# Window attention, forward and backward, on one core: from feature-major tiles with broadcast weights to token-major tiles with four shifts or four feature quarters on the partitions

## The chip, the cores and the metric

The kernel runs on one core of a Trainium2 chip. Times are device microseconds of one execution. The times of all the runs quoted are medians, and each ratio comes with a 95% interval.

## The reference, cut to what matters

One transformer layer (LayerNorm, window attention, LayerNorm, GELU feed-forward, residuals), and the gradients of its input and all its weights for a given output gradient. There are 2048 tokens of 512 features in 32 heads of 16; each token attends to 8 keys, 0, 2, ... 14 tokens back.

```
W, dil = 8, 2
idx = pos[:, None] - (jnp.arange(W) * dil)[None, :]        # masked where negative
kg, vg = k[:, :, idx], v[:, :, idx]                        # heads, tokens, 8, 16
logits = einsum("bhsd,bhswd->bhsw", q, kg) * scale
attn = softmax(logits)
o = einsum("bhsw,bhswd->bhsd", attn, vg)
h = x + o @ wo
h2 = h + gelu(LN(h) @ w1 + b1) @ w2 + b2
outputs: h2 and its vjp with respect to x, wqkv, wo, w1, b1, w2, b2
```

Attention thus has two dot products over the 16 features of a head (the logits; in the backward pass the gradient of the weights) and four weighted sums over the window of 8 (the output, dV, dQ, dK).

## The kernel before

q, k and v lie feature-major: a partition is one of 16 features of one of 8 heads, tokens run along the row, and a shift by 2 tokens is an offset in the row. An attention weight has to be multiplied into all 16 features of its head, so it must be repeated on 16 partitions. The weights are transposed, stored to DRAM, and read back 16 times over by a transfer with a leading step of zero:

```
def put_wh(eng, d_t, n, col0, src):                 # store of the transposed weights
    for b in range(2):
        d0 = d_t[0:H, 0:1]
        eng.dma_start(out=_ap(d0, [[n, 4], [W * n, H], [1, src.shape[-1]]], ...), in_=src[:, b, :])

def bcast(eng, out_t, d_t, g, n, w0):               # 16 copies, 8 heads, one row each
    b = d_t[8 * g:8 * g + 8, w0 * n:(w0 + WH) * n]
    eng.dma_start(out=..., in_=_ap(b, [[0, DH], [W * n, 8], [1, WH * n]]))
...
def b_gv(c):                                        # dV, one of the four sums
    for g in range(G):
        ps = acc(...)
        for w0 in (0, WH):
            bc = bl.tile([P, WH, HB], BF16, tag="bc", bufs=5)
            bcast(sync, bc, attn_b[c], g, HB, w0)
            nc.vector.tensor_tensor(out=bc[:], in0=bc[:], in1=over_w(gos[c][:, g, :], HB), op=ALU.mult)
            gather(ps, bc, w0, True)                # four 128x128 identity matmuls
```

The dot products multiply q by the shifted k on DVE and sum 16 partitions with matmuls of 8 columns.

## Time and profile before

| | before |
|---|---|
| time, median of 2 runs | 926.27 us (925.79 to 926.75) |
| first stage (forward) | 375.1 us |
| second stage (feed-forward backward) | 191.4 us |
| third stage (attention backward, dW1, dWo) | 297.3 us |
| fourth stage (dWqkv) | 60.4 us |
| start of the third stage to its first window sum | 15.6 us |

The stages are cut in the trace by events: the first matmul of the feed-forward backward pass, its last dW2 matmul, the last output of the LayerNorm gradient, and the end. The prediction below uses round bounds a microsecond or two away.

### The profile page before, as it was taken

How to read it: one execution, taken by the hardware profiler on the slowest of the kernel's cores; microseconds unless marked ns; L12 is line 12 of the kernel's file. 1: busy time of each engine (PE TensorE's matmuls, PEld its weight loads, DVE VectorE, ACT ScalarE, POOL GpSimd, SP SyncE). 2: the span in 40 equal slices, each digit the busy share in tenths (PEclk: the TensorE clock that was granted, in tenths of full speed). 3: DMA queues.
4: the chain of work that ended last, by engine and by line, in shares of the span. 5: the costliest groups of instructions: out<-in, count | busy, mean ns of one | idle time of the engine just before them, and what ended most of it. 6: DMA issues, size and time to landing. Idle time of an engine off the chain costs nothing.

```text
span 924.2 us, 12961 instructions
## 1 busy us (share of the span) xinstructions
PE 759.3 (82%) x4946; PEld 373.9 (40%) x4946; DVE 560.8 (61%) x914; ACT 442.3 (48%) x608; POOL 252.8 (27%) x342
## 2 busy tenths in 40 slices
PE   1855877779779688999999997599699799888498
PEld 1533434334334233444454544254345345333243
DVE  5538247765673636579878863739749649777200
ACT  3543534753734645688787764132352342343211
POOL 6321211540431657244343212302102110100400
PEclk9966787999989998999999999689899989999799
DMA  9445384673491899965565524997885966984651
GB/s 326 155 152 191 103 245 155 208 285 111 143 307 76 317 318 312 258 216 162 170 206 174 186 79 137 271 282 228 230 233 149 257 187 183 244 235 149 232 222 40
DMA packets 64764, 187.86 MB, mean 203 GB/s; under 512 B 9981, under 2 KB 23166, under 8 KB 64702
## 3 DMA queue, kind: packets, MB, share of 16 engines
q0 software_dynamic: 34144, 114.41, 37.5%
q1 hardware_dynamic: 30558, 72.63, 28.1%
q8 instruction: 38, 0.62, 0.3%
q14 instruction: 24, 0.20, 0.1%
HBM read 119.74 MB, written 67.23 MB: 202 GB/s over the span
## 4 chain that ended last, share of the span: by engine, by line
PE 29%; DVE 14%; issue 13%; DMA 12%; ACT 6%; POOL 4%; ACTq 0%; DVEq 0%; POOLq 0%
DMA bv<-attn_b 5%; PE psq L747 5%; PE psw L698 4%; DMA bg<-gl_b 4%; PE psy L674 4%; PE psw L496 3%; PE psg L531 2%; PE psk L624 1%; PE psx L552 1%; PE psv L624 1%; DVE bv L638 1%; DVE bg L658 1%; ACT bu L522 1%; PE pswo L709 1%; DVE by L523 1%
## 5 line engine op out<-in xcount | busy, mean ns | idle before, releaser
L364 PE MATMUL psf<-ln2T,w 128*128 128x512 bf16 x224 | 63.0, 426 | 19.4 <-ACT u L366 19.4
L624 PEld LDWEIGHTS <-ident 128*128 128x128 bf16 x384 | 37.3, 99 | 64.7 <-issue 19.9
L330 DVE TENSOR_TENSOR bc<-bc,v 128x2048 bf16<-128x2048 bf16 x32 | 38.8, 1222 | 36.4 <-DMA bc<-attn_f 36.3
L698 PE MATMUL psw<-h1tm,ln2a 128*128 128x512 bf16 (+1 forms) x256 | 59.2, 355 | 1.2 <-ACT ow L701 1.2
L674 PE MATMUL psy<-wqkvT,gt 128*128 128x512 bf16 x192 | 54.7, 415 | 5.3 <-DVE lua L475 5.2
L600 DVE TENSOR_TENSOR bp<-go,bv 128x2048 bf16<-128x2048 bf16 x32 | 36.8, 1221 | 36.3 <-ACT go L595 36.3
L299 DVE TENSOR_TENSOR pr<-q,k 128x2048 bf16<-128x2048 bf16 x32 | 37.3, 1219 | 35.0 <-ACT q L283 30.5
L531 PE MATMUL psg<-goutT,w2T 128*128 128x512 bf16 x224 | 57.9, 379 | 0.1
L638 DVE TENSOR_TENSOR bv<-bv,go 128x2112 bf16<-128x2112 bf16 x32 | 39.7, 1253 | 29.9 <-DMA bv<-attn_b 27.0
L382 PE MATMUL ps<-w,g 128*128 128x512 bf16 x224 | 53.8, 388 | 3.9 <-ACT u L366 2.1
L747 PE MATMUL psq<-gqa,ln1a 128*128 128x512 bf16 x192 | 44.5, 397 | 11.3 <-DMA gqa<-gq_d 11.3
L496 PE MATMUL psw<-gout,gtm 128*128 128x512 bf16 x224 | 53.1, 379 | 0.0
L281 PE MATMUL psq<-ln1T,wqkv 128*128 128x512 bf16 x192 | 49.7, 410 | 4.1 <-ACT ln1T L217 3.7
L552 PE MATMUL psx<-w1T,gh 128*128 128x512 bf16 x224 | 52.3, 379 | 0.5 <-DVE luf L475 0.5
L332 PE MATMUL pso<-bc,ident 128*128 128x512 bf16 x128 | 37.4, 419 | 9.3 <-DVE bc L330 9.3
L402 ACT COPY wT<-ptw 128x1024 bf16<-128x1024 bf16 (+1 forms) x23 | 22.4, 975 | 44.8 <-DMA w1T_d<-wT 15.3
L364 PEld LDWEIGHTS <-w 128*128 128x128 bf16 x224 | 23.4, 107 | 50.6 <-issue 34.3
L366 ACT ACTIVATE u<-psf,b1c 128x512 bf16<-128x512 f32 x56 | 37.1, 687 | 13.7 <-PE psf L364 9.3
L657 DVE TENSOR_TENSOR bh<-bg,bk 128x2048 bf16<-128x2048 bf16 x32 | 38.5, 1218 | 8.4 <-DMA bg<-gl_b 6.9
L372 ACT ACTIVATE s<-z 128x1024 bf16<-128x1024 bf16 x28 | 29.4, 1054 | 28.9 <-DVE z L370 16.3
L533 DVE CUSTOM_DVE_ANT_0 gh<-psg,by 128x512 bf16<-128x512 f32 x56 | 37.3, 686 | 8.2 <-PE psg L531 7.3
L624 PE MATMUL psv<-bv,ident 128*128 128x512 bf16 x128 | 34.7, 415 | 7.6 <-DVE bv L638 7.6
(206 smaller groups left out, 1625.1 us busy)
## 6 DMA issues: line engine op xcount, KB each, us to landing
bv<-attn_b SPq DMA_DIRECT2D x32, 528.0 KB, 6.7
bg<-gl_b SPq DMA_DIRECT2D x32, 528.0 KB, 11.5
bc<-attn_f SPq DMA_DIRECT2D x32, 512.0 KB, 11.4
x_d<-u POOLq DMA_DIRECT2D x28, 256.0 KB, 5.5
s_d<-s POOLq DMA_DIRECT2D x28, 256.0 KB, 4.2
g_d<-g POOLq DMA_DIRECT2D x28, 256.0 KB, 4.3
bu<-x_d POOLq DMA_DIRECT2D x28, 256.0 KB, 3.7
bs<-s_d POOLq DMA_DIRECT2D x28, 256.0 KB, 4.4
```

Source lines behind the costliest of these rows:

```text
L281: nc.tensor.matmul(ps[:], lhsT=wqkv[:, dc, jt * P:(jt + 1) * P], rhs=ln1T[:, dc, :], start=(dc == 0), stop=(dc == DC - 1))
L330: nc.vector.tensor_tensor(out=bc[:], in0=bc[:], in1=back_w(v[:, g, PAD:HB], CH, w0), op=ALU.mult)
L364: nc.tensor.matmul(ps[:], lhsT=w1[:, dc, ft * P:(ft + 1) * P], rhs=ln2T[:, dc, :], start=(dc == 0), stop=(dc == DC - 1))
L382: nc.tensor.matmul(ps[:], lhsT=gs[ft // 2][:, ft % 2, j * P:(j + 1) * P], rhs=w2[:, ft, :], start=(ft == 0), stop=False)
L496: nc.tensor.matmul(ps[:], lhsT=gtm[:, t, :], rhs=gout[t // TC][:, t % TC, :], start=(t == 0), stop=(t == NT - 1))
L531: nc.tensor.matmul(ps[:], lhsT=w2T[:, dc, ft * P:(ft + 1) * P], rhs=gT[:, dc, :], start=(dc == 0), stop=(dc == DC - 1))
L552: nc.tensor.matmul(ps[:], lhsT=gh1[ft // 2][:, ft % 2, j * P:(j + 1) * P], rhs=w1T[:, ft, :], start=(ft == 0), stop=(ft == FT - 1))
L624: nc.tensor.matmul(ps[:], lhsT=ident[:], rhs=src[:, w, o:o + CH], start=(w0 + w == 0), stop=(w0 + w == W - 1))
L638: nc.vector.tensor_tensor(out=bc[:], in0=bc[:], in1=over_w(gos[c][:, g, :], HB), op=ALU.mult)
L674: nc.tensor.matmul(ps[:], lhsT=gts[c][sel][:, g, j * P:(j + 1) * P], rhs=wqkvT[:, sel * G + g, :], start=(n == 0), stop=(n == NJ - 1))
L698: nc.tensor.matmul(ps[:, 0:nf * P], lhsT=ln2a[:, t // TC, t % TC, dc * P:(dc + 1) * P], rhs=tmx[:, t, 0:nf * P], start=(t == 0), stop=(t = ...
L747: nc.tensor.matmul(ps[:], lhsT=ln1a[:, t // TC, t % TC, dc * P:(dc + 1) * P], rhs=gqt[:, t // TC, t % TC, :], start=(t == NT - 1), stop=(t ...
```

## The change

The intent is to drop the 96 broadcasts and the long identity matmuls. q, k, v and the weights are kept token-major in DRAM. A tile's 128 partitions are 4 x 32 rows of 64 tokens. For a weighted sum the four are four shifts of the same rows; for a dot product they are the four feature quarters. A matmul with a 128 x 32 selector then adds the four, and four such matmuls fill the 128 partitions of a PSUM tile.

```
-    def bcast(eng, out_t, d_t, g, n, w0): ...
-    def gather(ps, src, w0, sh): ...               # 128x128 identity matmuls
-    def logits(lg, pr, g, w0): ...                 # 8-column matmuls
+    def half_rows(ap2d, c, f, pad=0):
+        return _ap(ap2d, [[2 * n, Q4], [TPR * n, PR], [1, 2 * n]], ...)
+    def put_rows / get_rows                        # q, k, v, go, gl, attn; x, outputs: leading 4
+    def row4(pool_, d_t, t0, nj, name, tag, bufs, shift):
+        for j0 in range(0, nj, 5):
+            nn = min(5, nj - j0)
+            sync.dma_start(out=t_[:, j0:j0 + nn, :],
+                           in_=_ap(d_t[:, :], [[abs(shift) * n, Q4], [TPR * n, PR], [1, nn * n]], ...))
+    def att4 ...                                   # weights, 128 B pieces, 4 transfers of 32 partitions
+    def feat4 ...                                  # feature quarters, 256 B pieces, 4 transfers
+    def dots(...):                                 # DVE 128x4096 products, then
+        nc.tensor.matmul(lg[PR * n:PR * n + PR, ...], lhsT=sel4[:], rhs=pr[...])
+    def wsum(...):                                 # DVE 128x2048 products, then
+        nc.tensor.matmul(ps[PR * n:PR * n + PR, :], lhsT=sel4[:], rhs=prs[wh][:, n, :], ...)
...
-    b_ga(3); b_sm(3); b_gv(3)                      # then the loop, with take(wg, ...) between
+    b_go(0); take(wg, 1); b_go(1); b_ga(0); take(wg, 1); b_go(2); b_ga(1)
+    for c in range(NC): take(wg, 1); b_sum(c, 2); take(wg, 1); b_sum(c, 0); ...
```

dW1 goes in halves of 256 columns (448 matmuls for 256).

## The prediction

> **What bounds the kernel now.** I read the page's shares first, then a table of stretches that I cut where the stages change, then the costliest groups, then the DMA issues and the DMA rows of two short windows.
>
> ```profile
> PE 759.3 (82%) x4946; PEld 373.9 (40%) x4946; DVE 560.8 (61%) x914; ACT 442.3 (48%) x608; POOL 252.8 (27%) x342
> ...
> 0.00:374.00 374.00, 275.82 (x1804) 135.89 (x1805) 211.66 (x349) 186.28 (x250) 140.26 (x195) 0.88 0.64 213
> 374.00:566.50 192.50, 183.93 (x1189) 92.99 (x1188) 141.96 (x324) 143.13 (x178) 57.45 (x78) 1.00 0.57 172
> 566.50:865.00 298.50, 255.07 (x1763) 125.61 (x1761) 207.16 (x241) 105.45 (x169) 43.15 (x54) 0.93 0.78 218
> 865.00:924.00 59.00, 44.51 (x192) 19.42 (x192) 0.00 (x0) 7.47 (x13) 11.92 (x16) 0.88 0.47 174
> ```
>
> The columns of the stretches are their length, the busy time of PE, PEld, DVE, ACT and POOL, the granted clock, the DMA share and GB/s. Four stages follow each other: forward (374 us), FFN backward (192.5), attention backward with the dW1 and dWo products (298.5), dWqkv (59). The change lies in the first and the third. The third is nearly full on PE (255 of 298.5 us, 85%), and DVE (69%) and DMA (0.78) are not far behind: no single wait can be taken away for much.
>
> ```profile
> L330 DVE TENSOR_TENSOR bc<-bc,v 128x2048 bf16<-128x2048 bf16 x32 | 38.8, 1222 | 36.4 <-DMA bc<-attn_f 36.3
> L638 DVE TENSOR_TENSOR bv<-bv,go 128x2112 bf16<-128x2112 bf16 x32 | 39.7, 1253 | 29.9 <-DMA bv<-attn_b 27.0
> L332 PE MATMUL pso<-bc,ident 128*128 128x512 bf16 x128 | 37.4, 419 | 9.3 <-DVE bc L330 9.3
> L624 PE MATMUL psv<-bv,ident 128*128 128x512 bf16 x128 | 34.7, 415 | 7.6 <-DVE bv L638 7.6
> L290 PE MATMUL ga<-ind,bp 128*128 128x8 bf16 x512 | 17.6, 167 | 3.7 <-DVE bp L600 3.5
> ```
>
> The reader sees the work that the change re-shapes: products at 1.22 us for 2048 columns, sums over the window as 512 identity matmuls (pso, psv, psq, psk, 0.27 us each, 139.7 us together), 1024 eight-column matmuls for the dot products, and DVE waiting for the broadcasts.
>
> The last view settled the number for me: two stores of the same size and packet size, 128 KB in 128 pieces of 1 KB.
>
> ```profile
> DMA  0000000001311222333333222237515144788798
> ...
> attn_b<-aTa POOLq DMA_DIRECT2D x2, 128.0 KB, 6.1
> ...
> DMA  6992780799989794000000000870000000000000
> ...
> out_dram<-o SPq DMA_DIRECT2D x4, 128.0 KB, 1.7
> ```
>
> The first two lines are of 55 to 62 us, where the transposed weights attn_f and attn_b are stored; their DRAM pattern starts with a dimension of 4 (four steps of w or h, then 32 heads, then a row). For about 2 us the DMA share is 2 to 3 tenths. The last two are of 205 to 214 us, with output stores of 128 partitions x 1 KB: the share is 7 to 9 tenths while they run, and they land in 1.7 us instead of 6.1. In the DMA records an output store's 128 packets take 0.49 us with 12 in flight on average (267 GB/s); an attn_f store's 128 packets take 2.42 us with 3.4 in flight (54 GB/s). The second attn_f store was issued 0.6 us after the first and its packets began only when the first's had ended: both seem to use the same four engines.
>
> **What the Trainium skill says.** "DMA: Bandwidth & Descriptors", section "Why a DMA increments its semaphore by 16 and not by 1": the number of engines of a DMA is the largest k up to 16 that divides the slowest dimension of both patterns, and one issued from SP takes the lowest-numbered k. The 54 against 267 GB/s above agree. The same page, "Specifications", asks for at least 512 B per piece; here 512 B packets took 29 ns and 1 KB packets mostly 46, so small pieces cost more per byte but are not ruinous. "VectorE: DVE Perf Modes", "The perf-mode tier table": a bf16 tensor_tensor of 2048 takes 1224 ns; here 1219 to 1222. "TensorE: Matmul & The Clock Gate", "Part 3: Packing small matmuls": three column tiles of 32 columns at N=512 ran 2.38 times as fast; no run here shows it yet.
>
> **The change part by part.**
> DVE: the attention products keep their number of elements. 64 dot products of 2048 columns become 32 of 4096 (64 x 1.22 = 78 us against 32 x about 2.3 = 74), and 128 weighted products stay 128 (32 x 1.22, 32 x 1.25 and so on, 154 us together), of 2048 instead of partly 2112 columns, worth 2 us. The innermost runs are contiguous (32 or 128 elements), so I keep the rate. Softmax parts are unchanged. DVE gains some 6 us, all beside other work.
>
> PE: 512 identity matmuls (139.7 us) become 512 of 32 output columns, and 1024 small ones (34.9 us) become 256 of 512 columns. If four column tiles overlap about 3 times (an estimate from the page's 2.38 for three), the 768 cost 768 x 0.216 / 3 = 55 us instead of 175: 120 us less PE time, some 80 of it in the third stage, whose PE load falls to about 175 of 298. If they don't overlap, 768 x 0.216 = 166 us and nothing is gained. dW1 in halves of 256 columns is the same number of columns, a few us more of weight loads.
>
> DMA, bytes: the 96 broadcasts (50.6 MB) and 12 chunk reads (6.5 MB) go. In their place: 64 transfers of the four-shift rows, each 128 x 5,120 B = 655 KB (41.9 MB); 8 x 2 quarter-feature tiles (12 MB in 256 B pieces, 47,000 of them); 16 weight tiles (4.2 MB in 128 B pieces, 34,000). The bytes do not fall. At my estimate of 19 and 14 ns a packet (from 29 ns at 512 B and 46 at 1 KB) the small pieces cost 56 and 30 us of each engine over the kernel.
>
> DMA, engines: here I expect the damage. The four-shift read has the DRAM pattern 4 shifts x 32 rows x 5 KB against 128 partitions, so it runs on 4 engines, always the same, as attn_f did. A packet of 5,120 B: 4 KB took 159 ns at its quickest and 7 KB 272, so about 198 ns; attn_f's packets came every 2.42 x 4 / 128 = 76 ns per engine where an undisturbed one takes 46, so I add 30. 32 packets x 228 ns = 7.3 us per transfer, 14.6 us for a half chunk, for which DVE then has four products, 4 x 1.22 = 4.9 us: DVE will wait.
> Third stage: 48 transfers x 7.3 = 350 us on those four engines. The rest of their load: the stage has 234 us of packets per engine now, of which 122 are broadcasts and 23 chunk reads, leaving 89; plus 28 and 23 for the small pieces, 8 for the stores of go and gl, 22 for the dx stores, which also get a leading 4 and go out from SP; less 15 for less crowding. 350 + 155 = 505 us. The stage cannot end before these engines have done this, and of 298.5 us it becomes about 500: plus 200 us.
> First stage: 16 x 7.3 = 117 us; x read twice in 16 pieces of 256 KB with a leading 4, 3.8 us each, 60; out_0 in 8 such stores, 30; small pieces 36; what stays of the 239 us there now without the broadcasts (62) and the old x and output pieces (17), 160. Sum 403 us against 374: plus 35, since some of it lies at the wrong time.
> Second stage: unchanged. Fourth: its reads get 4 KB rows instead of 1 KB, worth perhaps 2 us of an 11 us wait.
> Sum: 926 + 200 + 35 - 2 = 1159; I say 1155.
>
> **The rivals.**
> (a) The four-shift reads spread over 16 engines after all (the lowering regroups the dimensions, or reads behave otherwise than the stores I have seen). Then 48 x 655 KB at the 200 GB/s of the broadcasts is 157 us in the third stage, PE falls to about 175 and DVE (205) is the bound: some 240 us instead of 298, with 5 or 10 gained in front. That makes about 865. Against it stand the two stores with exactly this pattern.
> (b) Confined, but the engines run nearer their best (198 ns) and the rest of the traffic falls between: 48 x 6.3 = 304 plus 120, a stage of 440; forward as it was: about 1075.
> (c) Confined, and the SP queue in its order makes it worse: it also carries output stores that wait for ACT (72.8 us in the stage now) and weight tiles that wait for a round trip of the softmax through DRAM; with two or three row buffers the four engines then stand idle at times: stage 560, forward plus 80, about 1270.
> (d) Column tiles don't overlap: with the engines of (a) busy elsewhere, PE stays at 255 and the time near 920; under my main theory it changes nothing, as PE has room.
>
> **Range and chances.** Confinement I hold for about nine in ten. Within it the spread is that of (b) and (c). Range 1000 to 1270 with 1155 in the middle of the confined cases; faster by over 2% 0.10 (a), within 2% 0.03 (d with a), slower 0.87.
>
> **What would show it.** Right: the four-shift reads land after 7 us or more each while the mean DMA share in the third stage is low (about 505 / 500 on four engines but near 150 / 500 on twelve, so 0.45 to 0.5 on average), DVE's longest waits are for these tiles, PE's share of the span falls below 70%, and the FFN backward stage keeps its 192 us. PE: groups of the 32-column matmuls with about 70 ns busy each show the overlap, 216 ns its absence. Wrong: landings of 3 to 4 us and a DMA share of 0.8 in the third stage mean (a); DVE products well over 1.22 us (or 2.4 for 4096 columns) mean that the broadcast operand lost its rate, which I don't count; a first stage longer than 420 us means that the trip of q, k and v through DRAM before the first dot product costs more than I allow.

## More of the kernel before

The order of the backward attention is: dot products and softmax gradient of the last chunk, its dV, and only then, between the later parts, some dW1 products taken from a list (`take`) as filler for PE.

From the page of the kernel before: how many packets the transfers were cut into, the chain that ended last by engine, and the issues of the broadcasts (number, size, median us from issue to landing).

```profile
DMA packets 64764, 187.86 MB, mean 203 GB/s; under 512 B 9981, under 2 KB 23166, under 8 KB 64702
...
PE 29%; DVE 14%; issue 13%; DMA 12%; ACT 6%; POOL 4%; ACTq 0%; DVEq 0%; POOLq 0%
...
bv<-attn_b SPq DMA_DIRECT2D x32, 528.0 KB, 6.7
bg<-gl_b SPq DMA_DIRECT2D x32, 528.0 KB, 11.5
bc<-attn_f SPq DMA_DIRECT2D x32, 512.0 KB, 11.4
```

The chain is PE first and DMA fourth: transfers are many, but the work is mostly there when it is wanted. Half a megabyte lands 7 to 12 us after its issue, several of them in flight.

## The result and the profile after

| | before | after |
|---|---|---|
| time, median | 926.27 us | 1253.41 us (1251.89 to 1254.93, 2 runs) |
| first stage | 375.1 | 468.0 |
| second stage | 191.4 | 190.1 |
| third stage | 297.3 | 532.8 |
| fourth stage | 60.4 | 62.2 |
| third stage's start to first window sum | 15.6 | 71.9 |

The changed kernel is slower: the ratio is 1.3532 [1.3455, 1.3608]. A ratio here is the mean time of one kernel's fast runs over that of the other's of the same rounds, so it isn't quite the ratio of the medians. Its result is correct. Nearly all of the 327 us lies in the first stage (+93) and the third (+235).

From the page after: busy shares, packets, and the chain by engine and by line.

```profile
PE 748.6 (60%) x4306; PEld 343.8 (27%) x4306; DVE 561.2 (45%) x879; ACT 438.7 (35%) x600; POOL 238.9 (19%) x338
...
DMA packets 148199, 191.53 MB, mean 153 GB/s; under 512 B 100109, under 2 KB 107630, under 8 KB 148142
...
DMA 32%; PE 18%; issue 14%; SPq 13%; DVE 11%; ACT 6%; POOL 5%; POOLq 0%; ACTq 0%; DVEq 0%
```

DVE is busy for the same 561 us as before, PE for 11 us less, the bytes are 2% more. No compute engine got more work; the chain has moved from PE to DMA (12% to 32%) and to SP's sequencer (from nothing listed to 13%).

The same stretches after as the prediction shows of before: length, busy time of PE, PEld, DVE, ACT and POOL with instruction counts, granted clock, DMA share, GB/s.

```profile
0.00:468.00 468.00, 276.37 (x1399) 118.40 (x1400) 215.42 (x330) 186.51 (x248) 139.76 (x199) 0.79 0.59 173
468.00:658.00 190.00, 182.44 (x1181) 92.32 (x1178) 142.20 (x324) 142.36 (x177) 57.57 (x78) 1.00 0.55 166
658.50:1191.60 533.10, 244.90 (x1538) 113.48 (x1537) 203.58 (x225) 102.79 (x163) 33.16 (x45) 0.69 0.46 129
```

The third row carries the case. With the same DVE work in a stretch 1.8 times as long, the mean DMA share falls to 0.46 and yet the chain waits for DMA. That is what a few full engines among many idle ones look like in a mean.

The groups after that answer to those shown of before:

```profile
L279 DVE TENSOR_TENSOR pb<-ba,r 128x2048 bf16<-128x2048 bf16 x96 | 114.0, 1219 | 205.3 <-DMA r<-q_r 70.5
L285 PE MATMUL pss<-pb,sel 128*32 128x512 bf16 x384 | 51.5, 527 | 136.1 <-DVE pb L279 134.5
L262 DVE TENSOR_TENSOR pag<-go,bv 128x4096 bf16<-128x4096 bf16 x16 | 36.2, 2286 | 81.6 <-DMA go<-go_r 52.7
...
r<-go_r SPq DMA_DIRECT2D x16, 640.0 KB
```

The products run at their old rate (1219 ns for 2048 columns). DVE stands 205 us ahead of them waiting for the four-shift rows `r`, and PE stands 136 us behind DVE. The page gives no landing time for these reads, so I took them from the records of single packets, which carry a queue but no engine: in the third stage the number of row packets (5,120 B) in flight is exactly 4 for 266.6 us, 5 or 6 for another 19, and never more. One takes 226 ns on average (median 200), so 6,144 of them on four engines are 6,144 x 226 / 4 = 347 us. SP suffers too. In the third stage its issues of the tiles made of small pieces (`ba`, `bv`) take 2.0 to 2.9 us at the median and up to 16 us, where the old broadcasts were issued in about half a microsecond, and SP's issues together take 418 us of the stage's 533 (180 in e1 below). Full engines alone don't do this: in e8 below four engines are as full, but with pieces of 4,224 B, and each issue takes 0.60 us.

### The profile page after: what moved, and what is told of

Read it like the earlier page. It is cut to its first block, busy times and chain, and to the rows that moved or that the text cites. A ratio compares the mean times of both kernels' runs of the same rounds, so it can differ in the third digit from the quotient of the medians.

```text
span 1253.1 us, 11690 instructions
## 1 busy us (share of the span) xinstructions
PE 748.6 (60%) x4306; PEld 343.8 (27%) x4306; DVE 561.2 (45%) x879; ACT 438.7 (35%) x600; POOL 238.9 (19%) x338
## 4 chain that ended last, share of the span: by engine, by line
DMA 32%; PE 18%; issue 14%; SPq 13%; DVE 11%; ACT 6%; POOL 5%; POOLq 0%; ACTq 0%; DVEq 0%
DMA out_dram<-ow 8%; SPq L252 6%; DMA r<-q_r 5%; DMA r<-k_r 4%; SPq L243 4%; PE psq L734 4%; PE ps L389 2%; PE psw L509 2%; SPq L234 2%; DMA gout<-in_grad_out_dram 2%; DMA go<-go_r 1%; DMA v<-v_r 1%; DMA r<-go_r 1%; PE psw L677 1%; DVE pb L279 1%
## 5 line engine op out<-in xcount | busy, mean ns | idle before, releaser
L279 DVE TENSOR_TENSOR pb<-ba,r 128x2048 bf16<-128x2048 bf16 x96 | 114.0, 1219 | 205.3 <-DMA r<-q_r 70.5
L285 PE MATMUL pss<-pb,sel 128*32 128x512 bf16 x384 | 51.5, 527 | 136.1 <-DVE pb L279 134.5
L677 PE MATMUL psw<-h1tm,ln2a 128*128 128x256 bf16 x448 | 63.2, 291 | 52.7 <-ACT ow L680 52.7
L262 DVE TENSOR_TENSOR pag<-go,bv 128x4096 bf16<-128x4096 bf16 x16 | 36.2, 2286 | 81.6 <-DMA go<-go_r 52.7
L302 PE MATMUL psq<-wqkv,ln1T 128*128 128x512 bf16 x192 | 58.4, 465 | 24.0 <-ACT qkv L304 23.2
L649 PE MATMUL psy<-wqkvT,gT 128*128 128x512 bf16 x192 | 62.6, 478 | 3.7 <-DVE lua L488 3.3
L677 PEld LDWEIGHTS <-ln2a 128*128 128x128 bf16 x448 | 43.8, 103 | 72.3 <-issue 61.3
L262 DVE TENSOR_TENSOR pa<-q,k 128x4096 bf16<-128x4096 bf16 x16 | 36.3, 2284 | 54.2 <-PE lg L268 36.8
L279 DVE TENSOR_TENSOR pbo<-a,v 128x2048 bf16<-128x2048 bf16 x32 | 38.0, 1213 | 27.7 <-DMA v<-v_r 10.4
L304 ACT CAST qkv<-psq 128x512 bf16<-128x512 f32 x48 | 27.4, 588 | 48.2 <-PE psq L302 23.3
```

The source lines that it names most:

```text
L262: nc.vector.tensor_tensor(out=pr[:], in0=_ap(q_ap, [q_ap.ap[0], [P, 4], [0, W], [1, P]]), in1=_ap(k_ap, [k_ap.ap[0], [P, 4], [-DIL * P, W] ...
L279: nc.vector.tensor_tensor(out=pr[:].rearrange("p n (d h) -> p n d h", h=H), in0=_ap(a_ap, [a_ap.ap[0], [4 * H, 4], [0, DH], [1, H]], off=w ...
L285: nc.tensor.matmul(ps[PR * n:PR * n + PR, :], lhsT=sel4[:], rhs=prs[wh][:, n, :], start=(wh == 0), stop=(wh == 1))
L302: nc.tensor.matmul(ps[:], lhsT=ln1T[:, dc, j * P:(j + 1) * P], rhs=wqkv[:, dc, sel * D:(sel + 1) * D], start=(dc == 0), stop=(dc == DC - 1))
L649: nc.tensor.matmul(ps[:], lhsT=gts[c, sel][:, g, j * P:(j + 1) * P], rhs=wqkvT[:, sel * G + g, :], start=(n == 0), stop=(n == NJ - 1))
L677: nc.tensor.matmul(ps[:, i * 2 * P:(i + 1) * 2 * P], lhsT=ln2a[:, t // TC, t % TC, dc * P:(dc + 1) * P], rhs=tmx[:, t, :], start=(t == 0), ...
```

## The experiments

**The theory:** most of the loss is the confinement of transfers with a leading 4 to four DMA engines. **Its rivals:** (c) SP's queue in its order, blocked by output stores and weight tiles; (p) the small pieces; (t) the trips through DRAM of freshly computed rows; and a loss in the order of work that no transfer explains.

Times of all the runs, with the stages of their profiles (bounds as above; the last column is the time from the third stage's start to its first window sum):

| run | median us | ratio to before, 95% | stages 1 / 2 / 3 / 4, us | first sum |
|---|---|---|---|---|
| e1_spread | 1093.86 | 1.1769 [1.1727, 1.1811] | 442.3 / 193.0 / 389.3 / 61.8 | 89.2 |
| e1b_spread10 | 1099.66 | 1.1841 [1.1811, 1.1872] | 448.6 / 193.0 / 394.5 / 60.6 | 89.6 |
| e2_row_pool | 1169.37 | 1.2564 [1.2474, 1.2653] | 467.9 / 190.0 / 457.9 / 61.8 | 91.6 |
| e3_out_pool | 1239.52 | 1.3368 [1.3303, 1.3434] | 461.8 / 191.2 / 520.0 / 61.5 | 75.7 |
| e4_spread_outpool | 1088.66 | 1.1728 [1.1685, 1.1771] | 442.9 / 193.0 / 388.9 / 62.8 | 122.2 |
| e5_rows16 | 1068.68 | 1.1524 [1.1466, 1.1582] | 415.8 / 207.0 / 381.5 / 61.6 | 116.4 |
| e6_bigpieces (wrong result) | 1048.17 | 1.1288 [1.1243, 1.1334] | 407.5 / 192.8 / 380.4 / 61.4 | 88.3 |
| e8_before_k4 | 1109.89 | 1.1964 [1.1922, 1.2006] | 401.6 / 208.3 / 437.9 / 59.1 | 15.5 |
| e9_before_st16 | 926.82 | 1.0005 [0.9974, 1.0036] | 383.7 / 191.8 / 289.9 / 59.4 | 15.6 |
| e10_noround (wrong result) | 1076.6 | 1.1609 [1.1559, 1.166] | 419.6 / 207.7 / 385.0 / 61.5 | 120.0 |
| e11_big (wrong result) | 1054.19 | 1.1388 [1.1345, 1.1431] | 396.0 / 204.9 / 387.2 / 63.0 | 84.9 |
| e12_big_noround (wrong result) | 1052.76 | 1.1363 [1.1317, 1.1409] | 395.9 / 206.9 / 384.9 / 62.8 | 82.8 |

The four wrong results read other data to take a cost away, at the same shapes and amount of arithmetic.

### The four-shift reads spread: e1_spread and e1b_spread10

Each read becomes one transfer per shift, whose slowest dimension is 32 rows. Same bytes, same packets, four times the issues (in e1b, one of 10 tokens per shift: twice).

```
-            sync.dma_start(out=t_[:, j0:j0 + nn, :],
-                           in_=_ap(d_t[:, :], [[abs(shift) * n, Q4], [TPR * n, PR], [1, nn * n]], off=(t0 + j0) * n))
+            for s_ in range(Q4):
+                sync.dma_start(out=t_[PR * s_:PR * s_ + PR, j0:j0 + nn, :],
+                               in_=_ap(d_t[:, :], [[TPR * n, PR], [1, nn * n]], off=(t0 + abs(shift) * s_ + j0) * n))
```

> Changed kernel, but each four-shift read is cut into one transfer per shift (32 partitions x 5 KB, slowest dimension 32 on both sides, so 16 engines); the same bytes, four times as many issues on the SP queue (256 instead of 64). Main theory (the reads are confined to four engines that are always the same): third stage from 534 us to 240-310, first from 468 to 380-420, sum 870-960 us. Rival (the SP queue itself is the limit: its issues take long and it holds other work back in its order): more issues make it no better, 1150 us or more.

> As e1_spread, but one transfer per shift for all ten tokens (10 KB per partition), so 128 issues instead of 256. Main theory: as e1_spread within 2%. If the number of issues on SP matters, 3% or more below e1_spread.

Measured: 1093.86 and 1099.66 us, both correct. That is 160 us less than the changed kernel, 143.5 of it in the third stage and 25.7 in the first, and the number of issues hardly matters. The third stage of e1_spread, and its products:

```profile
635.70:1025.30 389.60, 233.58 (x1519) 111.16 (x1536) 206.51 (x225) 103.44 (x163) 33.14 (x45) 0.75 0.75 176
```

```profile
L280 DVE TENSOR_TENSOR pb<-ba,r 128x2048 bf16<-128x2048 bf16 x96 | 111.0, 1220 | 54.6 <-DMA ba<-gl_r 20.3
```

The same bytes now make a DMA share of 0.75 instead of 0.46, and DVE's idle time ahead of the products falls from 205.3 to 54.6 us. In the records up to 16 or 17 row packets are in flight. Confinement of these reads is confirmed, but only for half of the loss: the stage is still 92 us longer than before the change, and the 870 to 960 us that I expected were missed by more than 130. e1 relieves two things at once, the four engines and SP's blocked issues; e8 tells them apart.

### Other engines by another issuer: e2_row_pool

The row reads keep their pattern of 4 x 32 and are issued from POOL: `sync.dma_start` becomes `pq.dma_start` in `row4`.

> Changed kernel with the four-shift reads in their old form (slowest dimension 4) issued from the POOL queue instead of SP. Main theory: by the skill a POOL transfer of k=4 takes four consecutive engines from a moving cursor, so several reads run on different engines; third stage 330-430 us, sum 1000-1130. If a transfer of four engines were slow only for its own latency, or the time lay in the amount of bytes, 1200 us or more.

Measured: 1169.37 us, correct; above what I had expected of the main theory. (Its profiled run fell into the slow state, so its stages are some us too long; the other three runs are fast, with a median of 1162.09 us.) The records show 8, 12 and 16 row packets in flight, multiples of 4: successive transfers took different engines. (The rule that the expectation takes from the Trainium skill stands in "DMA: Bandwidth & Descriptors", "Why a DMA increments its semaphore by 16 and not by 1".) But packets took 527 ns instead of 226, and a new wait appeared, of POOL for a free row buffer. From its waits (us in total, times, longest):

```profile
POOL r L234 <- DVE pb L279: 106.6, 15, 22.5
```

So four engines per transfer are not a loss in themselves when the fours differ, but POOL's queue then stands in wait for DVE, with its other transfers behind it. It is a partial cure and not a clean test.

### SP's queue relieved of output stores: e3_out_pool and e4_spread_outpool

In e3 the stores of the layer's output, dx, dW1 and dWo go to POOL's queue, with the row reads confined as they were; e4 adds e1's edit.

```
-                sync.dma_start(out=dd.rearrange("(i p) f -> p i f", p=P), in_=...)     # dW1; likewise three others
+                pq.dma_start(out=dd.rearrange("(i p) f -> p i f", p=P), in_=...)
```

> Changed kernel, four-shift reads untouched on SP; the output stores of the first and third stage (out_0, dx, dW1, dWo) go to the POOL queue, so that they no longer wait behind the reads in SP's order, and out_0 and dx leave the four engines for some of the time. Main theory: the four engines still have 350 us of reads in the third stage, so only a little is gained: 1190-1245 us. Rival (head-of-line blocking in the SP queue, ACT's 119 us wait for these stores): 1130 us or less.

> Both changes of e1_spread (four-shift reads on 16 engines) and e3_out_pool (output stores moved from SP to POOL) together. Alone they gave -160 and -14 us. If the second cause is the order of the SP queue (in e1_spread SP stands for 102 us before the dx stores, and the next chunk's reads behind them), it shows only now, once the four engines are no longer the limit: third stage from 390 to 310-340 us, sum 1000-1045. If the two causes are independent, 1094 - 14 = 1080.

Measured: 1239.52 and 1088.66 us, both correct. Moving the stores alone gives 14 us, spreading alone 160, both 165. Rival (c) as the prediction told it, output stores at the head of SP's queue, is worth 5 to 14 us and falls as a main cause; its other half, weight tiles that wait for the softmax, is taken away in e10 and e12 below. My first guess for e4, 1000 to 1045 us, was missed. One caution: the edits also move instructions in PE's order. In the program order 192 of the 448 dW1 matmuls stand before the first window sum after the change and in e1, 221 in e3, and all 448 in e4, e5 and e10. The time to the first sum follows it (89.2 us in e1, 122.2 in e4), and after it the stage is shorter (300 against 267 us), so e4 against e1 isn't a pure test of the queue. Keep the pair in mind: the first sum came 33 us later and the stage was no longer (389.3 and 388.9), so time to the first sum isn't by itself time lost.

### The other transfers with a leading 4: e5_rows16

On e4, `put_rows` and `get_rows` (stores of q, k, v, go and the weights, reads of x and of the output gradient) also go as four transfers of 32 partitions. The stores of the layer's output and dx keep their leading 4.

```
         for f in range(2):
-            eng.dma_start(out=half_rows(ap2d, c, f, pad), in_=t_[:, 2 * f:2 * f + 2, :]...)
+            for s_ in range(Q4):
+                eng.dma_start(out=_ap(ap2d, [[TPR * n, PR], [1, 2 * n]], ...),
+                              in_=t_[PR * s_:PR * s_ + PR, 2 * f:2 * f + 2, :]...)
```

> As e4_spread_outpool, and the remaining transfers with a leading 4 (loads of x and grad_out, stores of q, k, v, go and of the two attention weights) cut into four of 32 partitions each as well, at the price of three more issues each on POOL and SP. If these confined transfers make the first stage long (DVE waits 42 us for x there): 20-50 us less than e4. If POOL's 0.7 us per issue takes it back: within 10 us of e4 or slower.

Measured: 1068.68 us, correct, 20 us less than e4. The first stage gives 27 and the third 7, and the second takes back 14. The second stage is 205 to 208 us in the profiles of e5, e8, e10, e11 and e12 and 190 to 193 in the others. The traces show where. e5 starts its second stage 27 us earlier than e4, but POOL issues the stage's first read of `bu` no earlier (at 428.5 us, e4 at 426.4), with 32 reads of the output gradient ahead of it in place of 8, and DVE is idle for 32.6 us until it can make its first `by` from it. So part of the 27 us was only moved into the next stage; e10, e11 and e12 look alike, and e8, which has the old reads, stays open. This is the fastest correct form of the changed kernel, and it is 15% slower than the kernel before.

### The small pieces: e6_bigpieces and e11_big

The quarter-feature tiles are read as one run per partition in place of 256 B pieces (e6, on e4). In e11, on e5, so are the weight tiles with their 128 B pieces. The same bytes are read from wrong places.

```
-                           in_=_ap(d_t[:, :], [[TPR * D, PR], [D, nj], [1, P]], off=t0 * D + P * s_))
+                           in_=_ap(d_t[:, :], [[TPR * D, PR], [1, nj * P]], off=t0 * D))
```

> As e4_spread_outpool, but the quarter-feature tiles are read as one contiguous run per partition instead of 256 B pieces: same bytes, 1,024 large packets in place of 47,000 small ones. The results are wrong on purpose. They hold each engine for 79 us in e1_spread; if that is on the path, 20-60 us less than e4; if the trips through DRAM and the order of the queue are what counts, within 15 us.

> As e5_rows16, with the small pieces of both kinds (256 B features, 128 B attention weights) read as one run per partition; same bytes, wrong on purpose. The 256 B pieces alone gave 40 us in e6; with the 128 B ones (29 us per engine more) 45-65 us less than e5, 1005-1025. If POOL and SP order are all that is left: as e5.

Measured: 1048.17 us, 40 less than e4; 1054.19 us, 14 less than e5. The pieces cost the first stage 35 us where its row transfers are still confined (442.9 to 407.5) and 20 where those are spread (415.8 to 396.0); the third stage moves by −8.5 and +6 and does not depend on them. So the two costs of the first stage overlap and may not be added. Rival (p) is real in the forward pass and nil in the backward. For e11 I had expected 1005 to 1025 us; that was missed.

### The trips through DRAM: e10_noround and e12_big_noround

The backward reads of fresh rows (`go_r`, `gl_r`) are taken from `v_r` and `at_r`, which were stored in the first stage: same sizes, nothing to wait for. e10 is on e5, e12 on e11.

```
-        go4 = feat4(bp, go_r, CJ * c, CJ, ...)
+        go4 = feat4(bp, v_r, CJ * c, CJ, ...)
-        d_a = at_r if sel == 2 else gl_r
+        d_a = at_r
-        ... (go_r, 0))[(1, 0, 2)[sel]]
+        ... (v_r, 0))[(1, 0, 2)[sel]]
```

> As e5_rows16, but in the third stage go is read back from the stored v and the softmax gradient from the stored attention weights: same bytes and pieces, wrong results on purpose, no wait for a trip of fresh data through DRAM. e5 has its first product of the stage 27 us and its first window sum 116 us after the stage's start (the kernel before: 5 and 16). If these trips are what is left: 40-80 us less than e5. If the stage is held by the transfers themselves: within 15 us of e5.

> e10 and e11 together, wrong on purpose. If confinement, small pieces and the trips through DRAM of the third stage account for the whole excess over the kernel before: 920-970. If more is missing (the first stage's own trips through DRAM): 970-1010.

Measured: 1076.6 us against e5's 1068.68, so nothing gained; 1052.76 against e11's 1054.19, the same, and far above the 920 to 1010 that I had expected. Rival (t) falls for the third stage. Yet the changed kernel waits up to 47.5 us for `go` in its waits. With the trip gone another wait took its place, as the waits of e12 show:

```profile
DVE pag L269 <- PE ga L275: 44.3, 3, 23.5
```

DVE makes the products `pag`, PE sums them into `ga`; DVE now waits for PE. The timeline of PE in e12, in the opening of its third stage (start, us, group; in brackets the idle time before it):

```profile
625.96 0.39 PE L275 MATMUL ga<-pag,sel 128*32 128x512 bf16 x2
629.40 5.16 PE L684 MATMUL psw<-h1tm,ln2a 128*128 128x256 bf16 x32 [3.05 <-DMA h1tm<-h1tm_d]
634.49 1.04 PE L275 MATMUL ga<-pag,sel 128*32 128x512 bf16 x14
...
656.30 5.37 PE L684 MATMUL psw<-h1tm,ln2a 128*128 128x256 bf16 x32 [6.08 <-DMA h1tm<-h1tm_d]
664.15 3.65 PE L684 MATMUL psw<-h1tm,ln2a 128*128 128x256 bf16 x32 [2.48 <-ACT ow L687]
676.52 5.38 PE L684 MATMUL psw<-h1tm,ln2a 128*128 128x256 bf16 x31 [8.72 <-DMA h1tm<-h1tm_d]
681.84 0.39 PE L275 MATMUL ga<-pag,sel 128*32 128x512 bf16 x2
```

And of DVE there:

```profile
655.81 4.49 DVE L269 TENSOR_TENSOR pag<-go,bv 128x4096 bf16<-128x4096 bf16 x2 [10.11 <-DMA r<-v_r]
660.22 2.35 DVE L286 TENSOR_TENSOR pb<-ba,r 128x2048 bf16<-128x2048 bf16 x2
685.43 0.69 DVE L620 TENSOR_TENSOR sp<-ga,attn 128x512 f32<-128x512 f32 x1 [22.85 <-PE ga L275]
```

The products for the second group of `ga` are done at 660.3 us. The matmuls that use them run at 681.8, behind dW1 filler that stands ahead of them in the program, itself waiting for its 1 MB tile `h1tm` while the DMA share is near 1:

```profile
653.00:663.00 10.00, 5.37 (x32) 4.02 (x33) 6.76 (x4) 0.00 (x0) 5.58 (x9) 0.66 0.97 267
663.00:673.00 10.00, 3.65 (x32) 3.02 (x31) 0.00 (x0) 1.17 (x2) 2.66 (x4) 0.85 0.98 237
```

Filler that waits is no filler. The kernel before has its first sum 15.6 us into the stage with no dW1 matmul ahead of it; e12 needs 82.8 us. The 67 us between them stand beside 88 us by which e12's third stage is still longer, but they are not a share of it: 236 of the 448 dW1 matmuls, 33 us of PE's time, are done in them, which the old kernel does later, and e1 against e4 shows such time given back. The waits of the filler for `h1tm`, 18 us, are loss as far as this trace shows. The rest is not shown: no run took the dW1 products out of the way, and the row buffers, three deep, the single buffers of the feature tiles (SP stands from 614.6 to 640.5 us for `pag` before it can read the next `bv`) and the low clock may have their share.

### The other way round: e8_before_k4 and e9_before_st16

The kernel before, with each broadcast as four transfers whose slowest dimension is 4 copies, so that each has at most four engines; the issues are four times as many, and nothing else is touched. And the kernel before with its confined stores of transposed weights spread.

```
# e8
-        eng.dma_start(out=out_t[:]..., in_=_ap(b, [[0, DH], [W * n, 8], [1, WH * n]]))
+        for d4 in range(4):
+            eng.dma_start(out=out_t[32 * d4:32 * d4 + 32]..., in_=_ap(b, [[0, 4], [W * n, 8], [1, WH * n]]))
# e9
-            eng.dma_start(out=_ap(d0, [[n, 4], [W * n, H], [1, ...]], ...), in_=src[:, b, :])
+            for w4 in range(4):
+                eng.dma_start(out=_ap(d0, [[W * n, H], [1, ...]], ...), in_=src[32 * w4:32 * w4 + 32, b, :])
```

> The kernel before, with nothing changed but the pattern of the broadcasts: each is four transfers of 32 partitions with a leading dimension of 4 instead of one with a leading 16; same bytes and packets. Confinement theory: 64 broadcasts of 540 KB in the third stage at about 85 GB/s, 6.3 us each, 400 us, beside 90 us of other packets: third stage 460-500 instead of 298, sum 1090-1160. If it is not the engine count that made the changed kernel slow: 920-960.

> The kernel before, with only its stores of transposed attention weights cut into four of 32 partitions (slowest dimension 32, so 16 engines, where now a leading 4 gives four): candidate for a version faster than both. These stores land in 6-7 us and stand before the broadcasts of f_o and of the q and k gradients; 2-3 us less for each of eight, at more issues: 0.3 to 1.5% faster, or the same if POOL's issues take it back.

Measured: e8 takes 1109.89 us, correct: confinement costs the old kernel 182 us, 141 of it in the third stage. In that stage exactly 4 packets of the broadcasts' size, 4,224 B, are in flight for 250 us. The additional issues are no rival of weight: SP's issues take 155 us of the stage's 437, and in e1, with four times the issues too, no cost showed against e1b. Its third stage and one of its waits:

```profile
610.30:1047.30 437.00, 289.91 (x1732) 131.02 (x1760) 210.22 (x240) 106.43 (x169) 43.26 (x54) 0.81 0.45 149
```

```profile
DVE bv L640 <- DMA bv<-attn_b: 101.7, 20, 13.0
```

It has the signature of the changed kernel (DMA share 0.45, clock 0.81, DVE waiting for the tile) without its layout, matmuls, small pieces or order. With e1 this shows the cause from both sides, here without SP being blocked. e9 takes 926.82 us against 926.28 of the kernel before in its rounds: the same. The confined stores that gave the clue cost nothing on balance (in the one profile the first stage is 8.6 us longer and the third 7.4 shorter). No version beats the kernel before.

## Why the prediction was right or wrong

**Direction and main cause: right.** The four-shift reads run on four engines. Predicted 228 ns a packet and 350 us for the 48 reads of the third stage; measured 226 ns and 347 us. The rest of the engines' load there was put at 155 us; the records give 244.7 us per engine on average, less a sixteenth of the row packets' time (86.8) makes 158; that is a mean of all sixteen, not the load of the four, so the agreement is rougher than it looks. The DMA share of 0.45 to 0.5 is 0.46, the second stage keeps its length (191.4 and 190.1), and PE's share falls below 70%. Rival (a) is refuted by the 4 packets in flight. The second stage keeps its clock of 1.00 too, so the change didn't slow the program as a whole.

**The total: inside the range, in part by luck.** The sum said 1155, and 1253 lies near the upper end, which was there for rival (c). Its numbers (third stage 560, first plus 80, about 1270) come closest to the measured 533, plus 93 and 1253, yet the stores that it blamed are worth 5 to 14 us. Two other costs filled its place: a first stage that I had sized too small, and a slow opening of the third that I had not seen. Both follow.

**The third stage: right in size, with one term missing.** I predicted plus 200 us, from load alone; it is plus 235. The load of 505 us is close to the 533, but e1 shows that load isn't the whole: with the reads spread the stage should have come near 300 and came to 389. Below the confinement lay a second delay that the sum has no term for, the slow opening. I had counted operations, not their order: that `go` takes a trip before its dot products and that dW1 filler had moved ahead of them stood in the diff. How the 92 us divide between the filler's place, the row buffers and the clock stays open.

**The first stage: the mis-sized term.** "Plus 35" from a sum of 403 us on the four engines; measured plus 93. I treated a chain of small steps (store q, k and v, read them in quarters, multiply, store the weights, read them) as a load that packs. Each kind of transfer in it measures about as much as the whole allowance: 26 us for the row reads (e1), 27 for the other leading fours (e5 against e4, part of it only moved into the second stage), 20 to 35 for the 256 B pieces (e6, e11). e12 still stands 21 us over the kernel before. The prediction named this as what a stage over 420 us would mean; the trips of q, k and v were not taken out by themselves. Nor was another part of the change that I had not counted as a wait: x has one buffer where it had three, and DVE waits 38.1 us for it, against 4.9 before and 21.9 in e12.

**PE: right that it has room, wrong in the amount.** Predicted 120 us less PE time; measured 11. The 32-column matmuls do overlap: at full clock in e12 twelve more `ga` matmuls take 1.04 − 0.39 = 0.65 us, 54 ns each. But in the changed kernel the 768 were busy for 96.4 us and not 55 (pss 51.5, pso 15.8, lg 15.7, ga 13.4), 126 ns each, so the sign I gave, about 70, failed as well. Other matmuls got slower in turn: the same 192 dx matmuls took 54.7 us before and 62.6 after. The granted clock of the third stage fell from 0.93 to 0.69. The Trainium skill, "TensorE: Matmul & The Clock Gate", section "HAM oscillation — how this bites in real kernels", says that waits for DMA between short groups of matmuls let the clock drop to half each time; the trace agrees: PE waits 36 times for DVE's products, 134.5 us in all, and the granted clock falls to half 20 times in the third stage and stays there for 335.6 of its 533 us, against 40.9 of 298 before. A starved PE pays twice, and my 120 us assumed an undisturbed clock.

**DVE: right.** 1.219 us for 2048 columns and 2.286 for 4096, as predicted; broadcasting the operand inside the instruction cost no rate. Busy time in all is 561 us in both; the 6 us less that I forecast didn't show.

**Smaller terms.** In the third stage the 256 B and 128 B pieces took 24.6 and 13.4 ns a packet against my 19 and 14. The fourth stage came out 1.8 us longer, not 2 shorter. Two readings of the prediction were loose and move no sum: the 6.1 us to landing belong to a store issued by POOL, so the fair pair is the two stores from SP, 2.42 against 0.49 us; and the 96 broadcasts are 51.4 MB by the sizes shown, not 50.6.

**Rival (c): its wait exists, its weight doesn't.** SP's sequencer holds 13% of the chain and its issues block for up to 16 us, but e3 gives 14 us, and e8 has the loss without the blocking. (e1's page lists 2% for SP, but its chain adds up to 29% of the span against 99% here, so the two can't be compared.) How much the blocked issues add to the full engines in the changed kernel is not shown.

**The account of the 327 us**, then: about 160 for the four-shift reads (e1), 20 for the other leading fours (e5), 14 to 40 for the small pieces (e11, e6). The remaining 100 to 130 are not settled: 126 us separate the profiles of e12 and before, 88 of them in the third stage, 21 in the first and 15 in the second.

## What to carry to other kernels

Read the slowest dimension of every DMA pattern before counting bytes: four rows ahead of 32 put a transfer on four engines here, and a low mean DMA share (0.46) beside a chain that waits for DMA (32%) was its sign; the cure is one transfer per outer index. When a layout change also reorders the work, write down what stands ahead of the first critical operation on each engine, since filler whose own data is late delays what stands behind it. And to prove such a cause, put it into the old kernel as well as taking it out of the new one.

## What the Trainium skill lacked or had wrong

- "DMA: Bandwidth & Descriptors", "Rules for kernel authors", has the rule right that a short outermost dimension confines a transfer, and the page gives a bandwidth per engine, but no measured rate or cost of such a transfer. Here four engines moved a 640 KB read in 6.4 to 13.3 us from its first packet to its last, about 8.1 at the median (81 GB/s), where before 54 GB/s came of 1 KB packets; the whole program lost 20% to it (e8) and 13% of the changed kernel's time came back by spreading (1253.41 to 1093.86, e1).
- The same page, "Issuing engines are not separate DMA queues", calls the sequencer's time to initiate a transfer usually small relative to the transfer. That failed here for tiles of small pieces while four engines were full: SP's issues then took 2.0 to 2.9 us at the median and up to 16 us, against about 0.5 before, and SP's sequencer was 13% of the chain. With pieces of 4,224 B on equally full engines (e8) an issue took 0.60 us.
- No page says that moving such reads from SP to POOL trades one wait for another: 8 to 16 packets in flight instead of 4, but 527 ns a packet instead of 226, and 106.6 us of POOL waiting for a free buffer (e2).
- "TensorE: Matmul & The Clock Gate", "Part 3: Packing small matmuls", has three column tiles at N=512 (2.38 times) and none with four column tiles alone. Here groups of four came to 54 ns a matmul at full clock (e12), where 128-column ones of N=512 go 215 ns apart ((1.89 − 1.03) / 4 us in the same trace), 4.0 times; but 126 ns each in the changed kernel, whose PE was starved.
